# A fused gated-attention and GELU-FFN kernel: two weight pieces fetched ahead of group 1's data, and one addition of the weight conversion done by a transfer

## The chip, the cores and the metric

The kernel runs on one core of one Trainium2 chip. A core has TensorE (PE in the profile; its weight loads are PEld), VectorE (DVE), ScalarE (ACT), GpSimd (POOL) and SyncE (SP), each with an instruction queue of its own that it works off in order, and 16 DMA engines that all queues share. The metric is the device time of one execution in microseconds, lower is better.

## The reference

A gated linear attention with a state of 48 x 48 for each head, over four sequences of 768 steps with eight heads, and behind it a GELU feed-forward layer without bias on the 3072 rows that result. Weights arrive as float64 and are brought to float32 pairs inside the kernel.

```python
for t in range(S):
    state = alpha[:, :, t, :, None] * state + np.einsum('bhd,bhe->bhde', k[:, :, t], v[:, :, t])
    y[:, :, t] = np.einsum('bhd,bhde->bhe', q[:, :, t], state)
...
x = np.ascontiguousarray(attn_out.transpose(0, 2, 1, 3)).reshape(B * S, H * D)
h = x @ w_in
g = 0.5 * h * (1.0 + erf(h * inv_sqrt2))
return (g @ w_out).astype(np.float32)
```

## The kernel before

**Attention.** The 3072 rows are 12 groups of 256 steps, three groups to a sequence. A group has two units of four heads, so there are 24 units; unit n belongs to group n // 2. A unit is loaded by SP in six transfers (decays `ad`, keys `kd`, queries `qd`, two each; with the second unit of a group also the values `vn`). On DVE its *scan part* (L254 to L258) and *back part* (L265, L268) form running products of the decays and scale queries and keys. PE then does *scores* (L284, and L293, which turns the keys), ACT copies the turned keys (`kn`, L300), DVE masks the scores (`ss`, L305), PE does *inside* (L322, L340), DVE sums the state (L357, L359) and carries it on (L364), PE adds the part of the older state, *outer* (L384). ACT casts the result into the feed-forward layer's input x (L426); for the first three groups PE subtracts the cast from the sum (L435) and ACT casts the rest (L441). A few rows of x are moved by six small transfers (L450, *spread*). ACT also checks the range of the decays twice for each unit (L165).

**Feed-forward layer.** The 2048 features are eight blocks. For group g and block f, GEMM1 is 18 matmuls into `hp` (L458), ACT applies GELU twice (L470, L471), the difference of the two is formed (DVE at L476, or PE and ACT at L480 and L484 while g < 3 early on), and GEMM2 is 12 matmuls into `acc` (L497). Evacuations of `acc` into `part` are L511 to L515. A block can be used once its two weight pieces, one of w_in and one of w_out, are converted.

**Weight pieces.** There are 16. Piece n is fetched by SP (L186, into one of three `st` buffers), then: ACT scales the upper half of each float64 (L197, `u`); DVE shifts it (L201), sets the sign (L205, giving `w`), takes the exponents (L215), forms the lower part (L220) and adds it (L230, *add*); ACT casts the sum to the high part (L233, `wih` or `woh`) and DVE subtracts that for the low part (L236, `wil` or `wol`). The lower part was written over the fetched data, which therefore stayed in use until the add.

**What sets the order.** A planner in the kernel (from `plan_unit` and `plan_piece` on) lays all steps out in time from a table of costs, ranks (the string `ORDER`, digits for units, letters for pieces) and dependencies, and the instructions of PE, DVE, ACT and SP are emitted in that order. POOL's follow the order of the program. So a change of ranks, costs or dependencies moves instructions everywhere, and each engine then waits, in its order, for what it needs.

Of the kernel before, what the change touches and what calls it, by code (L numbers as in the profile page):

```python
# [19 lines left out]
SIGN_EXP = -(1 << 23)  # L20
STAGE = 3
WARM = 22
# [8 lines left out]
)  # L31
ORDER = "0 1 2 3 a b c d e f 4 5 g h i j k l m n o p"


@with_exitstack
def gla_then_gelu_ffn(ctx: ExitStack, tc: tile.TileContext, q, k, v, alpha, qg, kg, ag, w_in, w_out, out):
# [154 lines left out]
    def conversion(n):  # L191
        _, hi, lo = pieces[n]
        d = {}

        def scaled():
            d["u"] = stage.tile([P, 2 * DM], F32, tag="u", bufs=1, name=f"u_{n}")
            nc.scalar.activation(d["u"], staged[n].bitcast(F32)[:, 1::2], AF.Copy, scale=2.0**-112)  # L197

        def shifted():
            ui = d["u"].bitcast(I32)  # L200
            nc.vector.tensor_scalar(out=ui, in0=ui, scalar1=3, scalar2=None, op0=ALU.logical_shift_left)  # L201

        def signed():
            d["w"] = stage.tile([P, 2 * DM], F32, tag="w", bufs=2, name=f"w_{n}")
            nc.vector.scalar_tensor_tensor(  # L205
                out=d["w"].bitcast(I32),
                in0=staged[n].bitcast(I32)[:, 1::2],
                scalar=SIGN,
                in1=d["u"].bitcast(I32),
                op0=ALU.bitwise_and,  # L210
                op1=ALU.bitwise_or,
            )

        def exponents():
            nc.vector.tensor_scalar(  # L215
                out=d["u"].bitcast(I32), in0=d["w"].bitcast(I32), scalar1=SIGN_EXP, scalar2=None, op0=ALU.bitwise_and
            )

        def rest():
            nc.vector.scalar_tensor_tensor(  # L220
                out=staged[n].bitcast(F32)[:, 1::2],
                in0=staged[n].bitcast(U16)[:, 1::4],
                scalar=2.0**-36,
                in1=d["u"],
                op0=ALU.mult,
                op1=ALU.mult,
            )

        def whole():
            nc.vector.tensor_tensor(out=d["w"], in0=d["w"], in1=staged[n].bitcast(F32)[:, 1::2], op=ALU.add)  # L230

        def high():
            nc.scalar.copy(flat(hi), d["w"])  # L233

        def low():
            nc.vector.tensor_tensor(out=flat(lo), in0=d["w"], in1=flat(hi).bitcast(F32), op=ALU.subtract)  # L236

        return scaled, shifted, signed, exponents, rest, whole, high, low
# [253 lines left out]
    def gemm2(g, f, ghi, glo, acc, first, last, done, n0=None):  # L492
        for k in range(2):
            for t in range(2):
                for j in range(2):
                    for a, w in (((ghi, wo_hi[f]), (ghi, wo_lo[f])), ((glo, wo_hi[f]),))[k]:
# [5 lines left out]
                            stop=(last and j == 1 and k == 1),  # L502
                        )
        if not last:
            return

        def evacuate():
            o = parts[0 if g == "s" else g % NSB]
            for t in range(2):
                if g in started:  # L510
                    nc.vector.tensor_tensor(out=o[:, t], in0=o[:, t], in1=acc[t], op=ALU.add)  # L511
                elif t == 1 and g == NG - 1:
                    nc.scalar.copy(o[:, t], acc[t])
                else:
                    nc.vector.tensor_copy(o[:, t], acc[t])  # L515
                if g == NG - 1:
                    nc.sync.dma_start(out[g * G + t * C : g * G + (t + 1) * C, :], o[:, t])
            started.add(g)
# [116 lines left out]
    def op(*args, **kw):  # L635
        ops.append(Op(*args, **kw))
        return ops[-1]
# [4 lines left out]
    def plan_unit(n):  # L642
# [10 lines left out]
        old = unit.get(n - NB * NU, {})  # L653
        d["load"] = op("SP", "load", lambda: load_data(g, u), [old.get("outer"), old.get("scores"), old.get("c0"), old.get("c1")] + ([unit[n - NB * NU].get("inside")] if old else []), rank=r - 30, lands=2.8)
        d["scan"] = op("DVE", "scan", start, [d["load"], p.get("q"), p.get("back")], rank=r)
# [11 lines left out]
        d["outer"] = op("PE", "outer", lambda: outside_part(g, u), [d["chain"]], rank=r)  # L667
        if g < NSB:
            for what in ("scores", "inside", "outer"):
                d[what].cost *= SLOW  # L670
# [23 lines left out]
    def plan_piece(n):  # L694
# [3 lines left out]
        r = piece_rank[n]  # L698
        d["get"] = op("SP", "fetch", lambda: fetch(n), [q3.get("c4")], rank=r - 30.5, lands=4.5)
        d["u"] = op("ACT", "u", fns[0], [d["get"], p.get("c3")], rank=-0.5)  # L700
        d["c0"] = op("DVE", "c0", fns[1], [d["u"]], rank=r)
        d["c1"] = op("DVE", "c1", fns[2], [d["c0"], wops.get(n - 2, {}).get("lo")], rank=r)
        d["c2"] = op("DVE", "c2", fns[3], [d["c1"]], rank=r)
        d["c3"] = op("DVE", "c3", fns[4], [d["c2"]], rank=r)
        d["c4"] = op("DVE", "c4", fns[5], [d["c3"]], rank=r)
        d["hi"] = op("ACT", "hi", fns[6], [d["c4"]], rank=-0.4)
# [6 lines left out]

    steps, plan = [], []
    next_f = [0] * NG
# [39 lines left out]
    def gemm1_op(g, t):  # L755
# [4 lines left out]
        if st["first"]:  # L760
            if prev:
                prev["last"] = True
                prev["evac"] = Op("DVE", "part", lambda p=prev: p["out"](), [prev["gemm2"]], rank=-2)
                waiting["DVE"].append(prev["evac"])
            state["run"] += 1
# [163 lines left out]
```

## Time and profile before

| | us |
|---|---|
| median of three runs | 541.49 |
| fastest and slowest of them | 539.23, 543.62 |
| the profiled execution | 538.57 |
| its span, first to last instruction | 537.0 |
| PE busy in the span | 511.0 |
| DVE busy | 302.4 |
| ACT busy | 210.1 |
| POOL busy | 38.6 |

Mean durations of some operations from the profile's groups, in ns:

| operation | ns |
|---|---|
| ACT L470 and L471, GELU | 599 and 595 |
| ACT L197, scaling of a piece | 917 |
| ACT L233, cast of a piece | 837 |
| ACT L300, copy kn | 586 |
| ACT L165, one check, and its read | 722 and 192 |
| ACT L426, cast of x and of z | 482 and 372 |
| DVE L305, mask | 682 |
| DVE L236, low part of a w_out piece | 986 |
| DVE L254 and L265, one scan each of two | 677 and 803 |

Times in the profile count from the span's start. "Busy" leaves the instructions that only issue transfers out. In the timeline a row has its start, its length, the engine, the line of the kernel, what it writes and reads, and in brackets how long its engine was idle before and what ended that. A name like `SPq` is the queue of that engine issuing a transfer. The lines that the argument uses stand in the prediction.

### The profile page before, as it was taken

The page shows a single profiled execution, that of the slowest core. Times are in us where ns is not written, and L with a number is a line of the kernel's source. Part 1 is how long each engine was busy: PE and PEld are TensorE (multiplying, and loading weights), DVE is VectorE, ACT ScalarE, POOL GpSimd, SP SyncE. Part 2 cuts the span into 40 slices and gives each one's busy share as a digit, 9 for nine tenths or more (in the row PEclk, how much of TensorE's full clock was granted, in tenths as well). Part 3 has the DMA queues.
Part 4 walks back from the last instruction along what each step waited for, and adds up shares of the span by engine and source line. Part 5 has one row for each costly group of instructions (what it writes and reads, how often), then busy time and mean ns, then how long its engine had stood idle before and what let it go on. Part 6 is the DMA issues. An engine that isn't in the chain of part 4 may idle for free.

```text
span 537.0 us, 13927 instructions
## 1 busy us (share of the span) xinstructions
PE 511.0 (95%) x5993; PEld 495.7 (92%) x5993; DVE 302.4 (56%) x558; ACT 210.1 (39%) x407; POOL 38.6 (7%) x51
## 2 busy tenths in 40 slices
PE   6667899999999999999999999999999999999995
PEld 6557889999999999999999999999999999999995
DVE  8799999989996976878339145132131121211211
ACT  5347666655435444343243243233232222222221
POOL 5000000000001210111001000000000000000000
PEclk9557999999999999999999999999999999999999
DMA  5838655432004423334022020010010000000001
GB/s 169 287 110 224 180 181 170 129 118 89 1 1 125 151 84 97 99 106 134 0 81 84 2 79 12 1 40 9 1 40 6 0 31 2 30 0 1 31 1 34
DMA packets 20722, 39.49 MB, mean 74 GB/s; under 512 B 4112, under 2 KB 7616, under 8 KB 20656
## 3 DMA queue, kind: packets, MB, share of 16 engines
q1 hardware_dynamic: 19136, 33.93, 21.1%
q0 software_dynamic: 1232, 4.33, 2.4%
q8 instruction: 49, 0.80, 0.7%
q10 hardware_dynamic: 288, 0.30, 0.2%
q14 instruction: 17, 0.14, 0.1%
HBM read 31.46 MB, written 4.72 MB: 67 GB/s over the span
## 4 chain that ended last, share of the span: by engine, by line
PE 86%; DVE 5%; issue 1%; DMA 1%; ACT 1%; SPq 0%
PE hp L458 38%; PE acc L497 37%; PE ybank L384 4%; PE ybank L322 2%; PE s L293 2%; PE s L284 2%; PE ybank L340 2%; DVE state L359 1%; DVE w L205 1%; DVE st L220 1%; DMA qd<-in_qg_dram 1%; DVE rp L265 1%; SPq L153 0%; DVE pp L254 0%; DVE u L215 0%
## 5 line engine op out<-in xcount | busy, mean ns | idle before, releaser
L458 PE MATMUL hp<-x,wih 128*128 128x256 f32 x1152 | 214.1, 285 | 0.0
L458 PEld LDWEIGHTS hp<-x,wih 128*128 128x128 f32 x1152 | 183.5, 192 | 1.1
L458 PE MATMUL hp<-x,wil 128*128 128x256 f32 x576 | 163.3, 284 | 0.0
L476 DVE TENSOR_TENSOR glo<-hp,ghi 128x512 fp32r<-128x512 f32 x87 | 59.9, 688 | 177.5 <-ACT hp L471 177.5
L470 ACT ACTIVATE ghi<-hp 128x512 fp32r<-128x512 f32 x96 | 57.5, 599 | 232.1 <-PE hp L458 231.9
L497 PE MATMUL acc<-woh,ghi 128*128 128x384 f32 x384 | 131.3, 342 | 0.0
L497 PE MATMUL acc<-wol,ghi 128*128 128x384 f32 x384 | 128.6, 335 | 0.0
L458 PEld LDWEIGHTS hp<-x,wil 128*128 128x128 f32 x576 | 110.7, 192 | 0.0
L497 PE MATMUL acc<-woh,glo 128*128 128x384 f32 x384 | 82.1, 334 | 0.0
L497 PEld LDWEIGHTS acc<-woh,ghi 128*128 128x128 f32 x384 | 72.4, 188 | 0.8
L497 PEld LDWEIGHTS acc<-wol,ghi 128*128 128x128 f32 x384 | 72.4, 189 | 0.0
L497 PEld LDWEIGHTS acc<-woh,glo 128*128 128x128 f32 x384 | 67.9, 188 | 0.0
L471 ACT ACTIVATE hp<-hp 128x512 f32<-128x512 f32 x96 | 57.1, 595 | 0.0
L261 POOL TENSOR_TENSOR qd<-qd,pp 128x512 f32<-128x512 f32 x18 | 23.2, 1288 | 224.3 <-DVE pe L255 133.3
L265 DVE TENSOR_TENSOR_SCAN rp<-ad,rp,top 128x255 f32<-128x255 f32 x48 | 36.6, 803 | 0.1
L384 PEld LDWEIGHTS ybank<-qd,state 48*48 48x48 f32 x704 | 23.0, 128 | 12.9 <-DVE state L359 9.5
L384 PE MATMUL ybank<-qd,state 48*48 48x64 f32 x704 | 26.7, 229 | 8.2 <-DVE state L359 8.2
L359 DVE TENSOR_TENSOR state<-ybank,state 128x96 f32<-128x96 f32 x80 | 20.5, 256 | 18.3 <-PE ybank L340 16.1
L254 DVE TENSOR_TENSOR_SCAN pp<-ad,top 128x256 f32<-128x256 f32 x48 | 30.3, 677 | 0.0
L300 ACT COPY kn<-s 128x512 f32<-128x512 f32 x24 | 14.1, 586 | 31.3 <-PE ybank L340 25.5
L521 POOL DMA_DIRECT2D out_dram<-part x11 | 8.3, 752 | 237.4 <-DVE part L515 162.4
L322 PEld LDWEIGHTS ybank<-ss,vn 64*64 64x64 f32 x768 | 14.6, 144 | 11.6 <-DVE ss L305 4.1
(74 smaller groups left out, 428.7 us busy)
## 6 DMA issues: line engine op xcount, KB each, us to landing
st<-in_moe_w_in_dram SPq DMA_DIRECT2D x8, 768.0 KB, 5.2
st<-in_moe_w_out_dram SPq DMA_DIRECT2D x8, 768.0 KB, 4.8
ad<-in_ag_dram SPq DMA_DIRECT2D x48, 96.0 KB, 2.4
kd<-in_kg_dram SPq DMA_DIRECT2D x48, 96.0 KB, 2.3
qd<-in_qg_dram SPq DMA_DIRECT2D x48, 96.0 KB, 3.1
vn<-in_v_dram SPq DMA_DIRECT2D x12, 384.0 KB, 4.3
out_dram<-part POOLq DMA_DIRECT2D x11, 384.0 KB, 3.2
x<-z SPq DMA_DIRECT2D x63, 32.0 KB, 3.0
```

The lines of the kernel that those rows point to most:

```text
L254: nc.vector.tensor_tensor_scan(pp[:, i], at[:, i], top, MID, ALU.mult, ALU.min)
L261: nc.gpsimd.tensor_tensor(out=qt, in0=qt, in1=pp, op=ALU.mult)
L265: nc.vector.tensor_tensor_scan(rp[:, i, G - 2 :: -1], at[:, i, G - 1 : 0 : -1], top[:, 1:], rp[:, i, G - 1 :], ALU.mult, ALU.min)
L300: nc.scalar.copy(d["kn"], d["s"][:, :, 2 * C : 4 * C])
L322: nc.tensor.matmul(ybank[o, b, t : t + CS], lhsT=vn[r, c, e : e + DP], rhs=d["ss"][r, h, 2 * i + c, :], start=(i == 0 and c == 0), stop=(j ...
L359: d["chain"] = nc.vector.tensor_tensor(out=st[j + 1], in0=new, in1=st[j], op=ALU.add)
L384: ins = nc.tensor.matmul(ybank[r, b, t : t + CS], lhsT=states[u][j][r, i], rhs=d["qt"][r, i, j * CS : (j + 1) * CS], start=False, stop=Tru ...
L458: nc.tensor.matmul(hp[:, j, :], lhsT=a[:, j, i * P : (i + 1) * P], rhs=x[:, i, :], start=(j == 0 and i == 0 and n == 0), stop=(i == NK - 1 ...
L470: nc.scalar.activation(ghi, hp, AF.Gelu)
L471: nc.scalar.activation(hp, hp, AF.Gelu)
L476: nc.vector.tensor_tensor(out=glo, in0=hp, in1=ghi.bitcast(F32), op=ALU.subtract)
L497: nc.tensor.matmul(acc[t], lhsT=a[:, j, t * C : (t + 1) * C], rhs=w[:, j, :], start=(first and j == 0 and k == 0 and w is wo_hi[f]), stop= ...
```

## The change

It has five parts.

1. The loads of units 0 and 1 get ranks -40 and -39 and the first two pieces' fetches -33 and -32, so these fetches stand ahead of the loads of units 2 and 3 (group 1). `ORDER` puts pieces a and b ahead of units 2 and 3, c and d ahead of 4 and 5.
2. The add leaves DVE: `w` gets `u` added by a transfer from POOL's queue that accumulates. The lower part is now written into `u`, so the fetched data are free once it is formed, and `u` is in use until the transfer has landed.
3. Buffers: two `st` instead of three, two `u` instead of one, three `w` instead of two. The scaling of piece n now waits for the sum of piece n - 2 instead of the lower part of n - 1.
4. The first evacuation of each of the groups 0 to 2 goes to ACT.
5. The second of the two last stores is issued from ACT's queue. The planner's slow factor for PE holds for the first four units, no longer for six.

```diff
-STAGE = 3
+STAGE = 2
-ORDER = "0 1 2 3 a b c d e f 4 5 g h i j k l m n o p"
+ORDER = "0 1 a b 2 3 c d 4 5 e f g h i j k l m n o p"
...
-            d["u"] = stage.tile([P, 2 * DM], F32, tag="u", bufs=1, name=f"u_{n}")
+            d["u"] = stage.tile([P, 2 * DM], F32, tag="u", bufs=2, name=f"u_{n}")
-            d["w"] = stage.tile([P, 2 * DM], F32, tag="w", bufs=2, name=f"w_{n}")
+            d["w"] = stage.tile([P, 2 * DM], F32, tag="w", bufs=3, name=f"w_{n}")
...
             nc.vector.scalar_tensor_tensor(
-                out=staged[n].bitcast(F32)[:, 1::2],
+                out=d["u"],
                 in0=staged[n].bitcast(U16)[:, 1::4],
...
-            nc.vector.tensor_tensor(out=d["w"], in0=d["w"], in1=staged[n].bitcast(F32)[:, 1::2], op=ALU.add)
+            nc.gpsimd.dma_start(d["w"], d["u"], accum_op=ALU.add)
...
+        EARLY = tuple(range(NSB))
-                elif t == 1 and g == NG - 1:
+                elif g in EARLY or t == 1 and g == NG - 1:
                     nc.scalar.copy(o[:, t], acc[t])
...
-                    nc.sync.dma_start(out[g * G + t * C : g * G + (t + 1) * C, :], o[:, t])
+                    (nc.scalar if t else nc.sync).dma_start(out[g * G + t * C : g * G + (t + 1) * C, :], o[:, t])
...
-        d["load"] = op("SP", "load", lambda: load_data(g, u), [old.get("outer"), old.get("scores"), old.get("c0"), old.get("c1")] + ([unit[n - NB * NU].get("inside")] if old else []), rank=r - 30, lands=2.8)
+        d["load"] = op("SP", "load", lambda: load_data(g, u), [old.get("outer"), old.get("scores"), old.get("c0"), old.get("c1")] + ([unit[n - NB * NU].get("inside")] if old else []), rank=-40.0 + n if n < 2 else r - 30, lands=2.8)
-        if g < NSB:
+        if n < 4:
             for what in ("scores", "inside", "outer"):
                 d[what].cost *= SLOW
...
-        d["get"] = op("SP", "fetch", lambda: fetch(n), [q3.get("c4")], rank=r - 30.5, lands=4.5)
-        d["u"] = op("ACT", "u", fns[0], [d["get"], p.get("c3")], rank=-0.5)
+        d["get"] = op("SP", "fetch", lambda: fetch(n), [q3.get("c3")], rank=-33.0 + n if n < STAGE else r - 30.5, lands=4.5)
+        d["u"] = op("ACT", "u", fns[0], [d["get"], wops.get(n - 2, {}).get("c4")], rank=-0.5)
-        d["c4"] = op("DVE", "c4", fns[5], [d["c3"]], rank=r)
+        d["c4"] = op("POOL", "c4", fns[5], [d["c3"]], rank=r, lands=2.6)
...
-                prev["evac"] = Op("DVE", "part", lambda p=prev: p["out"](), [prev["gemm2"]], rank=-2)
-                waiting["DVE"].append(prev["evac"])
+                again = prev["g"] >= NSB or prev["g"] in evacuated
+                evacuated.add(prev["g"])
+                prev["evac"] = Op("DVE" if again else "ACT", "part", lambda p=prev: p["out"](), [prev["gemm2"]], rank=-2)
+                waiting[prev["evac"].eng].append(prev["evac"])
```

What the planner makes of it shows at three places. The first is ACT's queue from its first work on data (`st` are fetched weights, `s` the scores, `ad` the decays, `x` the layer's input); before:

```order
L300 COPY kn_0_275<-s_0_245 128x512
L165 ACTIVATE junk_319,outside<-ad_118,lo_b 128x512
L197 ACTIVATE u_321<-st_266 128x768
L165 ACTIVATE junk_323,outside<-ad_118,hi_b 128x512
L300 COPY kn_1_353<-s_1_328 128x512
L165 ACTIVATE junk_377,outside<-ad_118,lo_b 128x512
```

And ACT's queue at the same place now:

```order
L197 ACTIVATE u_270<-st_213 128x768
L197 ACTIVATE u_272<-st_223 128x768
L300 COPY kn_0_277<-s_0_249 128x512
L165 ACTIVATE junk_314,outside<-ad_118,lo_b 128x512
L165 ACTIVATE junk_318,outside<-ad_118,hi_b 128x512
L300 COPY kn_1_363<-s_1_322 128x512
```

The scalings of pieces 0 and 1 stand ahead of unit 0's copy; before, the first of them stood between the copies of units 0 and 1. On SP the two fetches stand in the same way right behind the values of group 0.

The second place is DVE's queue behind the mask of unit 0, with the sign step's `w` and the state sums; before:

```order
L305 TENSOR_TENSOR ss_0_277<-s_0_245,mask 128x512
L254 SCALAR_TENSOR_TENSOR pp_0_279<-ad_122,top 128x256 x2
L255 TENSOR_SCALAR pe_0_281<-pp_0_279 128x2
L256 RECIPROCAL rp_0_280<-pe_0_281 128x2
L258 TENSOR_TENSOR qd_124<-qd_124,pp_0_279 128x512
L265 SCALAR_TENSOR_TENSOR rp_0_280<-ad_122,rp_0_280,top 128x255 x2
L268 TENSOR_TENSOR kd_123<-kd_123,rp_0_280 128x512
L357 COPY state_1_146<-ybank 128x96
```

And DVE's queue at the same place now:

```order
L305 TENSOR_TENSOR ss_0_279<-s_0_249,mask 128x512
L201 TENSOR_SCALAR u_270<-u_270 128x768
L205 SCALAR_TENSOR_TENSOR w_316<-st_213,u_270 128x768
L215 TENSOR_SCALAR u_270<-w_316 128x768
L220 SCALAR_TENSOR_TENSOR u_270<-st_213,u_270 128x768
L357 COPY state_1_146<-ybank 128x96
```

Piece 0 takes the place of unit 2's scan and back parts. These now stand behind pieces 0 and 1, and behind them, ahead of unit 2's mask, both low parts.

The third place is PE's queue between the outer parts of units 1 and 2; before:

```order
L284 MATMUL s_1_480<-qd_124,kd_123 64x64 x16
L293 MATMUL s_1_480<-ident,kd_123 128x128 x4
L435 MATMUL ybank<-z_514,minus 128x128 x2
L435 MATMUL ybank<-x_408,minus 128x128 x2
L322 MATMUL ybank<-ss_0_462,vn_121 64x64 x16
L340 MATMUL ybank<-vn_121,kn_0_454 64x48 x16
L384 MATMUL ybank<-qd_124,state_0_145 48x64
```

And PE's queue at the same place now:

```order
L435 MATMUL ybank<-z_499,minus 128x128 x2
L435 MATMUL ybank<-x_378,minus 128x128 x2
L322 MATMUL ybank<-ss_0_478,vn_121 64x64 x16
L340 MATMUL ybank<-vn_121,kn_0_480 64x48 x16
L284 MATMUL s_1_555<-qd_124,kd_123 64x64 x16
L293 MATMUL s_1_555<-ident,kd_123 128x128 x4
L384 MATMUL ybank<-qd_124,state_0_145 48x64
```

The scores of unit 3 have moved from ahead of the subtraction to between the inside part and the outer part of unit 2.

More of the change, by code (lines that the diff above doesn't have):

```diff
@@ L698, in plan_piece @@
         r = piece_rank[n]
-        d["get"] = op("SP", "fetch", lambda: fetch(n), [q3.get("c4")], rank=r - 30.5, lands=4.5)
-        d["u"] = op("ACT", "u", fns[0], [d["get"], p.get("c3")], rank=-0.5)
+        d["get"] = op("SP", "fetch", lambda: fetch(n), [q3.get("c3")], rank=-33.0 + n if n < STAGE else r - 30.5, lands=4.5)
+        d["u"] = op("ACT", "u", fns[0], [d["get"], wops.get(n - 2, {}).get("c4")], rank=-0.5)
         d["c0"] = op("DVE", "c0", fns[1], [d["u"]], rank=r)
-        d["c1"] = op("DVE", "c1", fns[2], [d["c0"], wops.get(n - 2, {}).get("lo")], rank=r)
+        d["c1"] = op("DVE", "c1", fns[2], [d["c0"], wops.get(n - 3, {}).get("lo")], rank=r)
         d["c2"] = op("DVE", "c2", fns[3], [d["c1"]], rank=r)
         d["c3"] = op("DVE", "c3", fns[4], [d["c2"]], rank=r)
-        d["c4"] = op("DVE", "c4", fns[5], [d["c3"]], rank=r)
+        d["c4"] = op("POOL", "c4", fns[5], [d["c3"]], rank=r, lands=2.6)
         d["hi"] = op("ACT", "hi", fns[6], [d["c4"]], rank=-0.4)
@@ L712, in gla_then_gelu_ffn @@
         plan_unit(n)
-    steps, plan = [], []
+    steps, plan, evacuated = [], [], set()
     next_f = [0] * NG
```

## The prediction

> **What bounds the kernel now.** I read the busy times by stretch first, then the chain that ended last, then the timeline of the first 80 us. Columns of the stretches: length, PE, PEld, DVE, ACT and POOL busy, granted TensorE clock, DMA share, GB/s.
>
> ```profile
> 30.00:40.00 10.00, 6.18 (x128) 5.72 (x128) 9.78 (x17) 4.51 (x11) 0.00 (x0) 0.50 0.47 140
> 40.00:50.00 10.00, 6.95 (x65) 6.29 (x69) 8.85 (x18) 7.25 (x13) 0.00 (x0) 0.61 0.76 205
> ...
> 80.00:90.00 10.00, 10.00 (x153) 9.40 (x152) 9.83 (x17) 8.14 (x16) 0.00 (x0) 1.00 0.51 141
> ...
> 400.00:500.00 100.00, 100.00 (x709) 100.00 (x708) 18.87 (x29) 26.18 (x48) 1.45 (x2) 1.00 0.04 12
> ```
>
> From 80 us to the end PE is busy all the time at clock 1.00. Up to 50 us it is busy about two thirds, at half clock, and DVE is nearly full. So the time is a fixed amount of PE work behind a slow start, and the change can only gain or lose in the start, unless it makes PE wait later. The chain (start, length, what):
>
> ```profile
> 42.09 1.95 PE ybank L384 x32
> 44.04 4.07 PE hp L458 x18
> ...
> 77.00 2.15 PE hp L458 x18
> 79.55 2.14 PE acc L497 x12
> ```
>
> The first GEMM1 takes 4.07 us at half clock, a later one 2.15; a GEMM2 takes 2.14. I call the GEMMs by group and feature block, (0,0) the first. I follow the start of the changed kernel with durations from rows (and from the table of means ahead of this part), beside the old one, until both keep PE full. All is against the profiled execution, 538.57 us (span 537.0), 2.9 under the median of the runs, 541.49.
>
> **The change, part by part.** *First pieces ahead.* Two weight loads move on SP from behind the loads of units 2 and 3 (six pair-loads and a value load) to ahead of them, and on ACT both scalings (L197) now stand ahead of the copy kn of unit 0. That copy is waited for by the mask of unit 0 on DVE (both read one PSUM tile), and this by all behind it on DVE and by PE.
>
> ```profile
> 8.00 0.42 SPq L157 DMA_DIRECT2D vn<-in_v_dram  x1
> 13.31 0.69 DVE L268 TENSOR_TENSOR kd<-kd,rp 128x512 f32<-128x512 f32 x1
> 14.59 0.47 SPq L186 DMA_DIRECT2D st<-in_moe_w_in_dram  x1
> 21.24 0.89 ACT L197 ACTIVATE u<-st 128x768 f32<-128x768 f32 x1 [8.52 <-DMA st<-in_moe_w_in_dram]
> 22.74 0.57 ACT L300 COPY kn<-s 128x512 f32<-128x512 f32 x1
> 23.34 0.69 DVE L305 TENSOR_TENSOR ss<-s,mask 128x512 f32<-128x512 f32 x1 [3.48 <-ACT kn L300]
> st<-in_moe_w_in_dram SPq DMA_DIRECT2D x1, 768.0 KB, 6.6
> st<-in_moe_w_out_dram SPq DMA_DIRECT2D x1, 768.0 KB, 8.1
> ...
> st<-in_moe_w_in_dram SPq DMA_DIRECT2D x8, 768.0 KB, 5.2
> out_dram<-part POOLq DMA_DIRECT2D x11, 384.0 KB, 3.2
> ```
>
> In the old kernel ACT waits 8.52 us for the first weight load, and DVE 3.48 behind it. In the new one the second weight load is issued about 9.0 (after the value load at 8.00 and the first weight load). Landing took 8.1 us behind all other loads, 5.2 as the median; I take the middle, 6.65, since half as much is queued ahead: 15.65. Scaling 0.92, copy 0.57: the mask starts at 17.2. DVE is free from 14.0 (13.31 + 0.69), so it waits 3.2 us, at the ends 1.8 and 4.7. The old wait is gone, one of the same size stands earlier.
>
> *DVE up to the first GEMM.* One scan and back part of a unit, from the L254 to the next work, took 4.22; the four operations of a piece 3.05:
>
> ```profile
> 14.52 1.26 DVE L254 TENSOR_TENSOR_SCAN pp<-ad,top 128x256 f32<-128x256 f32 x2
> ...
> 18.74 0.25 DVE L357 COPY state<-ybank 128x96 f32<-128x96 f32 x1
> ...
> 28.33 0.55 DVE L201 TENSOR_SCALAR u<-u 128x768 int32<-128x768 int32 x1
> ...
> 31.38 0.25 DVE L357 COPY state<-ybank 128x96 f32<-128x96 f32 x1
> ...
> L201 DVE TENSOR_SCALAR u<-u 128x768 int32<-128x768 int32 x16 | 9.8, 613 | 0.0
> L215 DVE TENSOR_SCALAR u<-w 128x768 int32<-128x768 int32 x16 | 8.9, 556 | 0.3
> L230 DVE TENSOR_TENSOR w<-w,st 128x768 f32<-128x768 f32 x16 | 15.3, 955 | 0.4
> L515 DVE COPY part<-acc 128x384 f32<-128x384 f32 x23 | 11.7, 550 | 3.3 <-PE acc L497 3.3
> ```
>
> From the mask of unit 0 to that of unit 2 stand now: three masks 2.0, two pieces 6.1, two state sums 2.2 (four operations of about 0.27 each), a carry 0.25, one scan part 4.22, two low parts 1.9: 16.7, so unit 2's mask ends at 33.9. The adds of both pieces (L230, 0.955 each) are gone from this list; they are transfers now. ACT then has copy, check, two casts, check, two rests:
>
> ```profile
> 35.27 0.73 ACT L165 ACTIVATE junk<-ad,hi_b 128x512 bf16<-128x512 f32 x1
> 37.04 0.38 ACT L441 CAST x<-ybank 128x256 fp32r<-128x256 f32 x1
> 14.66 1.14 PE L322 MATMUL ybank<-ss,vn 64*64 64x64 f32 x32 [3.40 <-DMA ad<-in_ag_dram]
> 17.49 1.11 PE L293 MATMUL s<-ident,kd 128*128 128x128 f32 x4
> ```
>
> 0.6 + 0.9 (the check with its read) + 0.75 + 0.9 + 0.75 = 3.9: unit 2's rests end at 37.8 (old: 37.42). PE now runs inside(2) and scores(3) in a row, 3.94 as from 14.66 to 18.60, then outer(2), 1.95: GEMM1 (0,0) starts at 43.7 against 44.04. **-0.3 us.** Unit 3's scan (DVE at 38.4) and state sum (41.1) are in time.
>
> *The clock.* The old PE is idle before 42.09 and then works without a break:
>
> ```profile
> 36.70:42.00 5.30, 2.05 (x65) 1.85 (x64) 5.06 (x12) 1.88 (x4) 0.00 (x0) 0.50 0.92 273
> 42.09:44.00 1.91, 1.91 (x33) 1.76 (x33) 1.11 (x2) 1.88 (x5) 0.00 (x0) 0.50 0.85 202
> ...
> 47.00:47.50 0.50, 0.50 (x4) 0.50 (x4) 0.50 (x1) 0.00 (x0) 0.00 (x0) 0.50 0.72 209
> ...
> 48.00:49.00 1.00, 0.33 (x3) 0.12 (x2) 1.00 (x2) 0.87 (x2) 0.00 (x0) 1.00 0.05 18
> 48.13 0.60 ACT L470 ACTIVATE ghi<-hp 128x512 fp32r<-128x512 f32 x1 [1.94 <-PE hp L458]
> 58.76 0.50 PE L458 MATMUL hp<-x,wih 128*128 128x256 f32 x2
> ```
>
> The clock came up 5.4 to 5.9 us after that start. In the new order PE works without a break from 37.8, so it is up by 43.7 and GEMM1 (0,0) takes 2.15 instead of 4.07. ACT's cast, check and table load (0.6, 0.9, 1.28) behind outer(2) end at 46.5; the first GELU starts there, not at 48.13. **-1.3 us more**; nothing if the break-free run does not come about.
>
> *From there to GEMM1 (0,1).* GELU 1.1, rest 0.5, weight cast 0.85 end at 48.95; DVE, at 48.7, waits 0.25 for that cast, then low part, unit 4's back part (2.05), state sum (1.1): 53.0. Scores, outer, two casts and the subtraction on PE bring GEMM1 (0,1) to 55.85, old 58.76; but inside(4), 1.1, was done before it in the old order and is not in the new, and of the 2.9 - 1.1 = 1.8 the 1.6 above are part. **-0.2.**
>
> *PE filling up.*
>
> ```profile
> 58.76:65.20 6.44, 6.13 (x75) 5.85 (x72) 6.27 (x11) 3.38 (x6) 0.00 (x0) 1.00 0.63 198
> 65.20:72.00 6.80, 6.65 (x109) 5.91 (x111) 6.73 (x11) 3.93 (x8) 0.00 (x0) 1.00 0.46 150
> 72.00:77.00 5.00, 4.29 (x77) 3.91 (x71) 4.83 (x11) 3.91 (x8) 1.27 (x1) 1.00 0.56 174
> ```
>
> The old PE still lost 0.31 + 0.15 + 0.71 = 1.2 us here. In the new one outer(4) waits for its state sum: DVE 53.0 + scan 2.2 + mask 0.6 + carry 0.25 + low part 0.9 + back 2.05 + half a piece 1.5 + sum 0.8 = 61.3; PE is ready at 60.6. It loses 0.7, and behind that DVE is ahead. **-0.5.**
>
> *The sum by a transfer.* No add inside a transfer is in the trace. Nearest below: 384 KB from POOL's queue, 3.2. By bytes read (786,432, the addend and the sum's old value) it is nearest to a weight load, 5.2; the other end is that load's worst, 8.1. I take 5.2. Cover: piece 1's rest ends at 25.75 and its low part's turn on DVE comes at 32.0, so with the cast (0.85) 5.4 us are free; piece 2's, 42.6 to its cast's turn at 48.1, 5.5. POOL has nothing else up to there. At 5.2 it costs **0**; above, each microsecond costs about two. Queued behind such a wait on ACT are casts and GELUs, and PE behind them. The smaller piece buffer (two loads, not three) is covered too: piece 2's load goes out at 20.85, lands by 26.1, and its scaling's turn is then.
>
> The Trainium skill (SBUF — State Buffer, "Summary: rules for kernel authors") speaks against this part: descriptor generation for transfers from GpSimd is starved while DVE is in a 2x or 4x mode, and it advises another queue. Were L201 and L215 such operations and both in the way (0.61 + 0.56), by that rule the transfer would take 6.4, the two places would cost 1.0 and 0.9, and the sum would be -0.6 instead of -2.5. No add beside DVE is in this trace to decide it.
>
> *The rest.* Ten adds after 77 us and the first evacuations (L515, 2 x 0.55 each, now on ACT) leave a DVE that no one waits for once PE is full: 0. The two last stores now issue from two queues:
>
> ```profile
> 531.83 0.84 SPq L517 DMA_DIRECT2D out_dram<-part  x2
> ```
>
> Half of this issue, less ACT's later start: **-0.2.** Together -0.3 - 1.3 - 0.2 - 0.5 - 0.2 = **-2.5**: 536.1 for the profiled execution, 539.0 on the median.
>
> **Rivals.** *All of DVE's relief counts.* The old chain runs over DVE up to 75 us; if the new one does too, six adds (5.7) and one evacuation (1.1) come off it, and the stores' 0.2: -7.0, 534.5. For it: DVE full in the rows above. Against: by the walk ACT and PE end the waits near 37.8, 43.7 and 55.85.
>
> *The transfer is slow.* Place: woh of piece 1 and wih of piece 2 on ACT. At 8.1 us it costs 2.7 + 2.6: +2.8, 544.3. It decides, slower by 1%, from 9.4 us (4.0 + 3.9 - 2.5 = +5.4), 546.9; at 11 us 550. For it: a read, an addition and a write by a path that the trace has not timed, among loads at a DMA share near 0.9. Against: 3.2 for the same bytes stored.
>
> *Nothing moves.* If the clock does not come up early, -1.2: 540.3, the same class.
>
> **How the numbers follow.** A measurement here tells about 1% (5.4 us) from no change. The forecast, a small gain hidden in that, with -0.6 and +2.8 inside: 0.60. DVE's relief in full: 0.23, faster. Slow transfer past 9.4: 0.17, slower. Faster 0.23, same 0.60, slower 0.17. The time is 539.0. The range goes from the fast rival, 534.5, less 2 for the spread of the runs (539.23 to 543.62), to the slow one's threshold, 546.9: 532.5 to 547.0. The likeliest case alone spans -4 (the weight load landing in 5.2) to +2.8: 537.5 to 544.3.
>
> **What would show it.** Right: a DVE wait of about 3 us at the mask of unit 0, released by ACT's kn; the first GEMM1 at 43 to 45 us in about 2.2 us; PE full from about 61; no change after 82. The transfer's time to landing decides cost 0 or not: wrong if ACT's L233 waits for it. Wrong as well if the mask of unit 0 does not wait, or if PE waits for weights after 82 us.

## The result, and the profile after

| | before | after |
|---|---|---|
| median of the runs, us | 540.36 | 557.31 |
| lowest and highest, us | 539.18, 543.62 | 556.63, 558.1 |
| runs | 4 | 4 |
| span of the profiled execution, us | 537.0 | 555.5 |

The ratio is 1.0315, 95% interval 1.028 to 1.0351: 3.2% slower (the kernel before has one run more here than in the table of its times). The forecast was 539.0 us with a range of 532.5 to 547.0, so time and class were both wrong. Medians and ratios, here and below, are of fast runs; one slow run of e10, 988.0 us, is left out.

The stretches of the changed kernel (length, then PE, PEld, DVE, ACT and POOL busy, granted clock, DMA share, GB/s):

```profile
30.00:40.00 10.00, 4.42 (x63) 3.57 (x55) 6.08 (x13) 4.58 (x11) 0.00 (x0) 0.50 0.60 170
40.00:50.00 10.00, 8.11 (x157) 7.07 (x159) 9.67 (x18) 5.82 (x12) 1.44 (x2) 0.78 0.45 111
50.00:60.00 10.00, 6.97 (x112) 5.70 (x112) 6.07 (x14) 2.92 (x4) 0.29 (x1) 0.73 0.96 250
60.00:70.00 10.00, 9.23 (x148) 8.69 (x147) 6.77 (x16) 5.21 (x13) 0.00 (x0) 0.59 0.43 120
...
80.00:90.00 10.00, 10.00 (x172) 9.30 (x167) 6.63 (x13) 7.96 (x16) 1.29 (x1) 1.00 0.70 177
90.00:100.00 10.00, 8.87 (x108) 7.91 (x107) 8.09 (x16) 3.73 (x7) 2.98 (x3) 1.00 0.78 184
100.00:110.00 10.00, 7.83 (x81) 7.02 (x80) 8.34 (x12) 7.90 (x16) 0.86 (x1) 1.00 0.64 188
...
150.00:160.00 10.00, 8.55 (x60) 8.13 (x59) 5.96 (x8) 4.43 (x7) 0.07 (x1) 1.00 0.19 40
160.00:170.00 10.00, 7.37 (x42) 7.20 (x41) 3.78 (x7) 3.39 (x6) 0.78 (x1) 0.86 0.22 41
...
400.00:500.00 100.00, 100.00 (x782) 99.45 (x782) 20.99 (x36) 26.27 (x50) 2.19 (x3) 1.00 0.05 15
```

From 180 us on the two kernels look alike: PE full, clock 1.00. What differs lies ahead of that. The old PE was full from 80 us on. The new one loses 3.3 us between 90 and 110, 0.5 between 130 and 150 and 4.1 between 150 and 170, and the granted clock halves behind the last gap (0.86 in the row of 160 to 170, 0.97 from 170 to 180), which makes about 1.7 us more: 9.6 us after 80. The span grew by 18.5, so the other 8.9 were lost by 80 us. DVE, nearly full before, now has idle time in most stretches.

The waits of ACT up to 180 us (sum, times, longest), and the transfers' time from issue to landing:

```profile
ACT wih L233 <- DMA w<-u: 18.7, 6, 4.2
ACT woh L233 <- DMA w<-u: 14.7, 3, 7.0
ACT u L197 <- DMA w<-u: 12.1, 4, 5.6
```

```profile
st<-in_moe_w_out_dram SPq DMA_DIRECT2D x8, 768.0 KB, 6.9
w<-u POOLq DMA_DIRECT2D x16, 384.0 KB, 7.3
```

ACT stands 45.5 us before sums that have not landed: 33.4 before casts (L233), which need the sum itself, and 12.1 before scalings (L197), which need the buffer `u` that a sum still reads. Half of the sums take over 7.3 us, where the forecast took 5.2. The chain of waits shows how that reaches PE (start, length, what):

```profile
146.81 7.22 DMA w<-u
...
159.94 3.91 DMA w<-u
...
164.61 0.59 ACT ghi L470
...
167.02 3.88 PE acc L497 x12
```

The last piece's sum is issued at 159.94 and lands 3.91 us later. ACT stands 7.0 us before the cast of that piece, the longest of its waits above; the GELU behind the cast comes at 164.61, and the next GEMM2 at 167.02.

### The profile page after: what moved, and what is told of

The parts are those of the page before. It is cut to its first block, busy times and chain, and to the rows that moved or that the text cites. A ratio compares the mean times of both kernels' runs of the same rounds, so it can differ in the third digit from the quotient of the medians.

```text
span 555.5 us, 13974 instructions
## 1 busy us (share of the span) xinstructions
PE 518.4 (93%) x5993; PEld 498.9 (90%) x5993; DVE 282.6 (51%) x534; ACT 210.6 (38%) x413; POOL 53.3 (10%) x67
## 4 chain that ended last, share of the span: by engine, by line
PE 69%; DMA 2%; issue 1%; ACT 1%; DVE 0%; ACTq 0%
PE acc L497 30%; PE hp L458 30%; PE ybank L384 3%; DMA w<-u 2%; PE ybank L322 2%; PE s L293 2%; PE ybank L340 1%; PE s L284 1%; ACT ghi L470 0%; ACT hp L471 0%; DVE glo L476 0%; ACT part L514 0%; DVE part L512 0%; PE tp L869 0%; ACT wih L233 0%
## 5 line engine op out<-in xcount | busy, mean ns | idle before, releaser
L497 PE MATMUL acc<-woh,ghi 128*128 128x384 f32 x384 | 132.7, 346 | 5.0 <-DVE part L512 3.1
L497 PE MATMUL acc<-wol,ghi 128*128 128x384 f32 x384 | 130.2, 339 | 0.0
```

Of the source, the lines that this page charges most:

```text
L497: nc.tensor.matmul(acc[t], lhsT=a[:, j, t * C : (t + 1) * C], rhs=w[:, j, :], start=(first and j == 0 and k == 0 and w is wo_hi[f]), stop= ...
```

## The experiments

Each kernel was timed beside the kernel before on the same chip. The last column is the median less that of the kernel before timed along with it. The intervals leave 1 to 3 us on either side of each difference. Where two of them are set against each other below, it is done before rounding.

| kernel | what it is | median, us | ratio, 95% interval | difference, us |
|---|---|---|---|---|
| after | the change | 557.31 | 1.028 to 1.0351 | +17.0 |
| e1 | sums back on DVE | 544.94 | 1.0052 to 1.0103 | +4.6 |
| e2 | old order, sums by transfer | 559.23 | 1.0292 to 1.0405 | +18.9 |
| e3 | planner reckons 6.5 us | 547.95 | 1.0062 to 1.0177 | +7.7 |
| e4 | copy without addition | 547.23 | one run | +6.9 |
| e5 | new order alone | 541.92 | 1.0004 to 1.0045 | +1.8 |
| e6 | e1 with three buffers | 547.39 | 1.0085 to 1.0146 | +7.3 |
| e7 | evacuations and stores alone | 545.25 | 1.005 to 1.0112 | +5.1 |
| e8 | loads behind the sums | 558.89 | 1.0272 to 1.0362 | +18.8 |
| e9 | sums on DVE, order of after | 549.25 | 1.0154 to 1.0194 | +9.5 |
| e10 | evacuations alone, order of before | 540.04 | 0.9976 to 1.0015 | +0.3 |
| e11 | first six sums by transfer | 548.25 | 1.0131 to 1.0185 | +8.5 |
| e12 | last ten sums by transfer | 554.6 | 1.0235 to 1.0284 | +14.8 |
| e13 | e12, planner reckons 6.5 us | 547.45 | 1.011 to 1.018 | +7.9 |
| e14 | before without the sums | 536.2 | 0.9899 to 0.995 | -3.3 |
| e15 | e11 corrected in three points | 550.69 | 1.0154 to 1.0221 | +11.2 |

Only e4, e9, e10 and e14 keep a written order (e4 and e9 that of the changed kernel, e10 and e14 that of the kernel before). In the others the planner writes it anew, and two of those may differ by some microseconds for that alone, as e7 and e15 show below.

**Is it the transfer, or the rest of the change?** Theory A: the landing time of the transfers, and ACT behind it. Theory B: the early pieces, the buffers or the evacuations.

e1, sums back on DVE:

```diff
-            nc.gpsimd.dma_start(d["w"], d["u"], accum_op=ALU.add)
+            nc.vector.tensor_tensor(out=d["w"], in0=d["w"], in1=d["u"], op=ALU.add)
...
-        d["c4"] = op("POOL", "c4", fns[5], [d["c3"]], rank=r, lands=2.6)
+        d["c4"] = op("DVE", "c4", fns[5], [d["c3"]], rank=r)
```

> The changed kernel with the sum of each piece back on DVE (in place, 0.96 us each) and everything else of the change kept: early pieces, two staging buffers, evacuations on ACT, split last stores. Theory A (the transfer's landing time, 7.3 us median, and ACT's queue standing behind it, make the whole loss): 534 to 541 us, PE without a gap after 82 us, no ACT wait over 3.5 us at a weight cast. Theory B (the early pieces, the third staging buffer taken away or the evacuations on ACT make the loss): at least 550 us. In between, 543 to 549: both have a part.

544.94: 12.4 us of the 17.0 go away, and 4.6 stay. Theory A holds for the larger part. It is not all: it expected 541 at most and no gap of PE, and PE idles 1.9 us between 80 and 90.

e2, the old order with the sums by transfer:

```diff
-ORDER = "0 1 a b 2 3 c d 4 5 e f g h i j k l m n o p"
+ORDER = "0 1 2 3 a b c d e f 4 5 g h i j k l m n o p"
```

The ranks of the first loads are as before, too.

> The changed kernel with the old order of pieces and units and the old ranks of the first loads; sums by transfer, two staging buffers. Theory A: the time stays at 551 to 561 us, with the same ACT waits on the transfers. Theory B with the early pieces as its cause: 545 us or less.

559.23: the early pieces are not the cause of the loss. ACT waits for transfers there as well, 16.0 and 9.2 us at the two kinds of cast.

e9, every engine's order as in the changed kernel, only DVE adds where POOL issued (the planner's line stays):

```diff
-            nc.gpsimd.dma_start(d["w"], d["u"], accum_op=ALU.add)
+            nc.vector.tensor_tensor(out=d["w"], in0=d["w"], in1=d["u"], op=ALU.add)
```

> The changed kernel with every engine's written order kept as it is, the planner still reckoning a transfer, but each sum done by DVE at the place where the transfer was issued. Theory A (the transfer's 7.3 us from issue to landing make the loss): ACT's waits for sums shrink to under 8 us in all and the time falls to 541 to 547 us, as when the planner knows of DVE's sum (544.9). Rival (the order that the planner wrote for a 2.6 us transfer is bad by itself, whoever adds): 552 us or more.

549.25, between the two: 7.5 us less than the change without any new order. ACT waits for no transfer of a sum any more. PE still loses 1.7 us between 80 and 90, and more in two later stretches; in those DVE, which now has the sums and an order written without them, is full:

```profile
90.00:110.00 20.00, 17.98 (x169) 17.33 (x169) 19.59 (x28) 12.15 (x22) 2.59 (x2) 0.91 0.43 137
...
130.00:150.00 20.00, 17.80 (x115) 17.61 (x114) 19.67 (x28) 7.40 (x12) 0.90 (x1) 0.91 0.20 68
```

So the transfer costs 7.5 us in this order, and 12.4 with an order made for the one or the other.

**Which of the sixteen sums?** e11 sends the first six by transfer, e12 the last ten (there with `n >= 6`):

```diff
-            nc.gpsimd.dma_start(d["w"], d["u"], accum_op=ALU.add)
+            if n < 6:
+                nc.gpsimd.dma_start(d["w"], d["u"], accum_op=ALU.add)
+            else:
+                nc.vector.tensor_tensor(out=d["w"], in0=d["w"], in1=d["u"], op=ALU.add)
...
-        d["c4"] = op("POOL", "c4", fns[5], [d["c3"]], rank=r, lands=2.6)
+        d["c4"] = op("POOL" if n < 6 else "DVE", "c4", fns[5], [d["c3"]], rank=r, lands=2.6 if n < 6 else 0.0)
```

> The changed kernel with only the first six pieces summed by transfer, the last ten on DVE. With all sixteen PE was 8.9 us behind the kernel before at 80 us and lost 9.6 more after; with none it is 544.9. If both halves cost by themselves: 549 to 553 us. If lateness of the first six runs on into everything behind: 555 us or more. If only the last ten cost: 547 us or less.

> The changed kernel with only the last ten pieces summed by transfer, the first six on DVE. The forecast took nothing for these ten, since PE is full there. If that held: 547 us or less, as with none. If the last ten make PE run out of weights between 90 and 170 us by themselves: 550 us or more, with PE idle 4 us or more in that stretch.

Over e1, the first six cost 3.8 us and the last ten 10.2, together 14.0, where all sixteen cost 12.4. The larger part lies where the forecast took nothing; the 3.8 are not more than an order written anew can make (548.25 lies between what e11's theories expected). In e12 (columns as above; an inserted line moves L233 to L236):

```profile
110.00:130.00 20.00, 18.32 (x156) 17.52 (x154) 16.70 (x26) 10.69 (x20) 2.98 (x3) 1.00 0.59 151
130.00:150.00 20.00, 15.69 (x95) 15.51 (x96) 14.29 (x22) 9.19 (x16) 3.84 (x4) 0.89 0.59 147
```

```profile
ACT wih L236 <- DMA w<-u: 16.3, 5, 4.2
```

PE idles 1.7 and 4.3 us in stretches that were full before.

**ACT's order, or late pieces?** e3 has only the planner's number for the transfer changed, e13 the same for the last ten:

```diff
-        d["c4"] = op("POOL", "c4", fns[5], [d["c3"]], rank=r, lands=2.6)
+        d["c4"] = op("POOL", "c4", fns[5], [d["c3"]], rank=r, lands=6.5)
```

> The changed kernel with a planner that reckons 6.5 us from issue to landing of a sum, not 2.6: the order written for ACT then sets casts later and other work ahead of them. If the loss is ACT standing in order before a cast whose sum has not landed (45 us of such waits up to 180 us), those waits fall below 15 us and the time to 545 us or less. If the pieces themselves come too slowly, whatever stands ahead of them, the waits fall but PE still runs out of weights after 90 us: 549 to 557 us.

> The changed kernel with the last ten pieces summed by transfer and the planner reckoning 6.5 us for each, not 2.6. With 2.6 it took 554.6 us, 9.7 more than with none by transfer. If the 9.7 us are ACT standing in order before casts whose sums have not landed, 547 us or less. If the pieces come too late whatever the order: 551 us or more.

e3 takes 547.95: 9.3 us less than the change, by a number in the planner, with the sums landing in 6.6 us as a median. ACT stands before no cast any more, only before scalings that need a sum's buffer:

```profile
ACT u L197 <- DMA w<-u: 12.7, 4, 4.5
```

e13 takes 547.45, 6.9 less than e12. Most of the cost is thus ACT standing in order before casts that were written too early. e3's time lies between what its two theories expected, and e13's just above the bound of the first. What is left over e1 is 3.0 us for e3 and 3.3 for e13; that can be lateness of the pieces themselves or the order written anew, and no run tells these apart.

**Why does a sum take 7 us?** e4 copies and does not add:

```diff
-            nc.gpsimd.dma_start(d["w"], d["u"], accum_op=ALU.add)
+            nc.gpsimd.dma_start(d["w"], d["u"])
```

> The changed kernel with a plain copy in place of the adding transfer, same size, queue, place and waits; the addition is left out. If the addition inside the transfer makes it slow, the copy lands in a median of 3.2 to 4.5 us (the stores of 384 KB from the same queue take 3.2) and the time is 545 us or less. If the packets stand behind the weight load that is released by the same DVE operation, it lands in 6 to 7 us and the time is 552 us or more.

It landed in a median of 6.1 us, as the theory of the queue has it, but took 547.23 us, a time that this theory did not expect. Both have a share in the 7.3 us. The time fell much more than the landing, 10.1 us in the same written order (one run): ACT's waits before these transfers come to 29.8 us instead of 45.5, PE idles 3.9 us behind 80 us instead of 7.9, and the granted clock, once up, does not fall again while PE is full. It is 1.00 between 60 and 80 us, where the change has 0.79:

```profile
60.00:80.00 20.00, 18.59 (x329) 17.23 (x330) 18.18 (x35) 15.24 (x32) 2.36 (x3) 1.00 0.70 211
```

How the 10.1 us divide among these, no run shows. The queue's rows, of the change and of the copy (packets, MB, share of the 16 engines over the span):

```profile
q0 software_dynamic: 3536, 10.62, 8.1%
```

```profile
q0 software_dynamic: 2512, 10.62, 5.5%
...
w<-u POOLq DMA_DIRECT2D x16, 384.0 KB, 6.1
```

The stores alone are 2.4% of 537.0 us in the profile of the kernel before. Less those, a sum keeps all 16 engines busy for 2.0 us and a copy for 1.1; the fastest sum landed after 3.9 us, the fastest copy after 2.6. The rest is waiting. Packets around a sum issued at 106.71, half a microsecond behind a weight load released by the same DVE operation (L220): first from 107.25 to 109.50, then from 109.50 to 112.50; and a sum with nothing beside it, from 160.94 to 163.85:

```profile
q1 hardware_dynamic: 190, 0.58, 88.5%
```

```profile
q0 software_dynamic: 143, 0.39, 68.4%
q1 hardware_dynamic: 82, 0.20, 22.4%
```

```profile
q0 software_dynamic: 144, 0.39, 74.4%
```

While 190 packets of the loads' queue (q1) go, the sum (q0) gets none. The first packet of the lone one started 1.4 us after its issue, and it landed after 3.9. The other's first packet started 2.9 us after its issue, so it was held back for 1.5 us more; it then shared the engines with the rest of the load, and landed after 6.3:

```profile
st<-in_moe_w_in_dram SPq DMA_DIRECT2D x1, 768.0 KB, 4.9
w<-u POOLq DMA_DIRECT2D x1, 384.0 KB, 6.3
```

```profile
w<-u POOLq DMA_DIRECT2D x1, 384.0 KB, 3.9
```

The Trainium skill (DMA: Bandwidth & Descriptors, "Queues, rings and completion order") says that a DMA engine goes in turn between the queues it has work for, and drains a whole packet of one, typically 9 to 17 descriptors, before it switches. The 190 packets of the profile are 12 for each engine: if they are descriptors of the page, this is a single turn and the trace agrees; if they are its packets, it does not. No run here tells which.

e8 issues the loads from POOL too, each behind the sum:

```diff
-        nc.sync.dma_start(staged[n].rearrange("p (two e) -> p two e", two=2), pieces[n][0])
+        (nc.sync if n < STAGE else nc.gpsimd).dma_start(staged[n].rearrange("p (two e) -> p two e", two=2), pieces[n][0])
...
-        d["get"] = op("SP", "fetch", lambda: fetch(n), [q3.get("c3")], rank=-33.0 + n if n < STAGE else r - 30.5, lands=4.5)
+        d["get"] = op("SP" if n < STAGE else "POOL", "fetch", lambda: fetch(n), [q3.get("c3")], rank=-33.0 + n if n < STAGE else r + 0.1, lands=4.5)
```

> The changed kernel with the weight loads from the third on issued from POOL's queue, each behind the adding transfer that the same DVE operation releases. If the transfer lands late because the load's packets go ahead of it (packets of the add at 107 us began only when most of the load's were through), it lands in a median of 5 us or less, and the time falls to 553 us or less though the loads come later. If it is slow by itself or by the other loads, the median stays at 6.5 us or more and the time at 555 us or more.

```profile
w<-u POOLq DMA_DIRECT2D x16, 384.0 KB, 4.9
st<-in_moe_w_in_dram POOLq DMA_DIRECT2D x7, 768.0 KB, 8.3
st<-in_moe_w_out_dram POOLq DMA_DIRECT2D x7, 768.0 KB, 8.4
```

The sums land in 4.9 us, so the load ahead is most of what kept them. The time does not fall: the loads now take 8.4, and ACT's waits for loads are 29 us instead of 11.7. One of the two is late whichever goes first.

**The 4.6 us that are not the transfer.** e5 is the kernel before with the new order, with the new ranks of the first loads and the planner's slow factor for four units:

```diff
-ORDER = "0 1 2 3 a b c d e f 4 5 g h i j k l m n o p"
+ORDER = "0 1 a b 2 3 c d 4 5 e f g h i j k l m n o p"
```

> The kernel before with the new order alone: the first two pieces ahead of group 1's loads, their two loads issued behind unit 1's, three staging buffers, the sum on DVE, evacuations on DVE. With the sum on DVE the whole rest of the change lost 4.6 us, 0.77%. If the early pieces make that loss (the mask of unit 2 and GEMM1 (0,0) come later), 543 to 547 us. If the forecast's terms for this part hold (-0.3, -1.3, -0.2, -0.5), 536 to 540 us, and the loss lies with the buffers or the evacuations.

e6 is e1 with the old buffers, and with the dependencies on them:

```diff
-STAGE = 2
+STAGE = 3
...
-            d["u"] = stage.tile([P, 2 * DM], F32, tag="u", bufs=2, name=f"u_{n}")
+            d["u"] = stage.tile([P, 2 * DM], F32, tag="u", bufs=1, name=f"u_{n}")
...
-            d["w"] = stage.tile([P, 2 * DM], F32, tag="w", bufs=3, name=f"w_{n}")
+            d["w"] = stage.tile([P, 2 * DM], F32, tag="w", bufs=2, name=f"w_{n}")
```

> The changed kernel with the sum on DVE and the old buffers: three staging buffers, one u, two w. If the loss of 4.6 us comes from the third staging buffer taken away (ACT waits 17 us for weight loads in the first 180 us with two), 541 us or less and these waits below 10 us. If it comes from the order or the evacuations, 543 to 547 us.

e7 is the kernel before with the change's lines for the evacuations and the last stores, planned anew:

```diff
-                elif t == 1 and g == NG - 1:
+                elif g in EARLY or t == 1 and g == NG - 1:
...
-                    nc.sync.dma_start(out[g * G + t * C : g * G + (t + 1) * C, :], o[:, t])
+                    (nc.scalar if t else nc.sync).dma_start(out[g * G + t * C : g * G + (t + 1) * C, :], o[:, t])
...
-                prev["evac"] = Op("DVE", "part", lambda p=prev: p["out"](), [prev["gemm2"]], rank=-2)
+                prev["evac"] = Op("DVE" if again else "ACT", "part", lambda p=prev: p["out"](), [prev["gemm2"]], rank=-2)
```

> The kernel before with two parts of the change alone: each group's first evacuation on ACT (four of them), the last two stores from two queues. The forecast took 0 and -0.2: 539 to 541 us. If ACT, which holds the GELUs, is late by two evacuations of 0.86 us in a row there, 542 us or more.

The order costs 1.8 (between what e5's theories expected), the evacuations with the split stores 5.1, and the old buffers do not help (e6 is 2.6 slower than e1, in an order of its own). 1.8 and 5.1 are more than the 4.6 to be explained, so the parts do not add up. e10 then swaps the engine of the first evacuations and leaves every order as it was:

```diff
-                elif t == 1 and g == NG - 1:
+                elif g in range(NSB) or t == 1 and g == NG - 1:
```

> The kernel before with the first evacuations (three pairs of copies before all weights are there) on ACT at the same place of the written order; nothing replanned, last stores untouched. If ACT's time is what the evacuations cost (545.25 us when replanned): 543 us or more. If that loss came from the other order that the planner wrote, the time stays at 539 to 541.5 us.

540.04, no change. So ACT has the time for the evacuations; e7's loss most likely comes with the order that the planner wrote when one operation moved (the split stores, which e10 lacks, lie at the end of the span and were not tried alone). Where the 4.6 us lie stays open.

**What could be gained at all?** e14 leaves the sums out of the kernel before, in its written order:

```diff
-            nc.vector.tensor_tensor(out=d["w"], in0=d["w"], in1=staged[n].bitcast(F32)[:, 1::2], op=ALU.add)
+            pass
```

> The kernel before, same written order, with the sixteen sums on DVE left out (the lower part of each weight piece is not added). This is the most that taking the sum off DVE can bring in that order: sixteen times 0.955 us less on DVE, and a transfer of no time at all. If DVE's relief counts in full as the fast rival had it, 534 us or less. If PE is the bound from 80 us on and only the start can gain: 536 to 539.5 us.

536.2 us, 3.3 less; PE is full from 80 us on as before, and the gain lies ahead of that (between 40 and 60 us the granted clock averages 0.87, before 0.80):

```profile
40.00:60.00 20.00, 15.89 (x296) 14.46 (x295) 18.26 (x37) 14.22 (x27) 0.00 (x0) 0.87 0.77 211
80.00:90.00 10.00, 10.00 (x174) 9.28 (x172) 8.81 (x17) 7.25 (x14) 0.00 (x0) 1.00 0.47 158
```

e15 puts together what the runs spoke for: e11 with 6.5 us reckoned, evacuations (the diff of e7 undone) and last stores as before:

```diff
-        d["c4"] = op("POOL" if n < 6 else "DVE", "c4", fns[5], [d["c3"]], rank=r, lands=2.6 if n < 6 else 0.0)
+        d["c4"] = op("POOL" if n < 6 else "DVE", "c4", fns[5], [d["c3"]], rank=r, lands=6.5 if n < 6 else 0.0)
```

> The changed kernel with what the runs so far speak for: only the first six sums by transfer, the planner reckoning 6.5 us for them, evacuations on DVE and last stores as before. If the three corrections add up (3.3 us for the six, 2.8 and more for the evacuations as replanned, from 548.25): 540 to 543 us, level with the kernel before. If an order written anew costs its own few microseconds whatever is in it: 544 us or more.

550.69, and slower than e11. The corrections do not add up, and no version here that does all of the sums beats the kernel before.

## Why the prediction was wrong, point by point

**First pieces ahead, -0.3: the place was right, the sum was not.** The wait that the forecast set at the mask of unit 0 (3.2, ends 1.8 to 4.7) is there with 2.68, and the second load was in by 15.25, forecast 15.65. The start of the changed kernel:

```profile
16.72 0.69 DVE L305 TENSOR_TENSOR ss<-s,mask 128x512 f32<-128x512 f32 x1 [2.68 <-ACT kn L300]
...
20.78 1.28 POOL L230 DMA_DIRECT2D w<-u  x1 [12.31 <-DVE state L357]
...
25.27 1.11 SPq L186 DMA_DIRECT2D st<-in_moe_w_out_dram  x1
25.56 0.85 POOL L230 DMA_DIRECT2D w<-u  x1 [3.51 <-DVE u L220]
...
34.32 0.83 ACT L233 CAST woh<-w 128x768 fp32r<-128x768 f32 x1 [4.11 <-DMA w<-u]
...
36.05 0.68 DVE L305 TENSOR_TENSOR ss<-s,mask 128x512 f32<-128x512 f32 x1
...
40.51 1.13 PE L322 MATMUL ybank<-ss,vn 64*64 64x64 f32 x32 [0.74 <-ACT x L441]
...
45.40 0.50 PE L458 MATMUL hp<-x,wih 128*128 128x256 f32 x2
...
48.28 0.60 ACT L470 ACTIVATE ghi<-hp 128x512 fp32r<-128x512 f32 x1
...
53.98 0.83 ACT L233 CAST wih<-w 128x768 fp32r<-128x768 f32 x1 [4.10 <-DMA w<-u]
...
63.66 0.73 PE L458 MATMUL hp<-x,wih 128*128 128x256 f32 x2
```

Unit 2's mask ends at 36.73, not 33.9, because DVE stood behind the cast of piece 1, and that behind its sum. GEMM1 (0,0) starts at 45.40, forecast 43.7. With the sums on DVE its first matmul starts at 44.26 in e5, 0.3 us later than the old one at 43.97, not 0.3 earlier.

**The clock, -1.3: it was up in time, in part by luck, and the gain went elsewhere.** GEMM1 (0,0) ran at full clock and took 2.4 us by its matmuls' first start and last end, 4.13 before. But the run without a break that the forecast asked for did not come about: PE idled 0.74 us up to 40.51, and the granted clock was 0.50 until 44.3 us and full from there, 3.8 us behind that gap and not 5.4 to 5.9. And ACT, behind a copy, two checks, a cast and the table load, reached the first GELU at 48.28, not 46.5; before it was 48.13.

**The sum by a transfer, cost 0: this is the step that failed, first in its size.** The forecast took 5.2 us to landing, between 3.2 and 8.1, against a cover of 5.4 for piece 1 and 5.5 for piece 2. Piece 1's rest ended at 25.24 and its cast ran at 34.32: 9.1 us. Piece 2's ended at 45.23, the cast ran at 53.98: 8.8 us. Both overran the cover, by 3.7 and 3.3 us, and ACT stood 4.1 us each time. GEMM1 (0,1), forecast for 55.85, came at 63.66. The nearest rows were taken for size in bytes; that the same DVE operation releases a 768 KB load, which goes ahead, stood in the order and was not drawn on (the rows at 25.27 and 25.56).

As far as e1, in an order of its own, can show, what such an overrun costs was priced about right. By the forecast's own rule these two are 7.0 us. The change stands 8.9 us behind the kernel before at 80 us, and e1, with the sums on DVE, about 2.7 (its span is 6.3 us longer, and some 3.6 of that come behind 80), so the transfers made about 6.2 there. And 541.49 - 2.5 + 7.0 = 546.0 is still inside the range: the time left it by the next term.

**The rest, ten more adds at 0: the same step failed a second time, and for more.** The words "a DVE that no one waits for once PE is full" looked at the engine that was relieved. The engine that was burdened is ACT: its queue holds each cast ahead of GELUs, so a sum that lands later than the planner thought can delay PE. The change itself said `lands=2.6` for its planner; the forecast took 5.2 and did not ask what an order written for 2.6 does at the other places. The last ten cost 10.2 us (e12 over e1), of which 6.9 went when the planner reckoned with the landing (e13). In the change 9.6 us were lost behind 80 us. The evacuations' 0 was right for the instructions (e10) and not for the kernel (e7): the forecast did not price that the whole order is written anew.

**The rule that was weighed.** By the Trainium skill (SBUF — State Buffer, "Summary: rules for kernel authors") descriptors for POOL's transfers are starved beside some DVE operations, which would have made 6.4 us. The first sum was issued at 20.78, the row above, with an operation on DVE inside that time that may be of that kind (0.55 us, where L220 takes 0.96 for as many elements). So was the third, at 45.53. Behind these rows stand the issue times of all sixteen (ns, least, median and most):

```profile
21.41 0.55 DVE L201 TENSOR_SCALAR u<-u 128x768 int32<-128x768 int32 x1
...
45.53 0.90 POOL L230 DMA_DIRECT2D w<-u  x1 [19.11 <-DVE u L220]
45.75 0.55 DVE L201 TENSOR_SCALAR u<-u 128x768 int32<-128x768 int32 x1
```

```profile
L230 POOL DMA_DIRECT2D w<-u x16: 828/850/1276, 20.8 to 159.9; - x16
```

The trace bears the rule out at most once: the first issue took 1.28 us where the median is 0.85, the third 0.90 with the same operation wholly inside it. That is 0.4 us, in one of sixteen. The 7.3 us are near the 6.4 for another reason, the load ahead: without that the sums land in 4.9 (e8).

**The rivals.** "The transfer is slow" named the place (ACT's L233) and the sign. Its price was wrong: +2.8 at 8.1 us and 550 only at 11, since it counted two of sixteen places; at a median of 7.3 the change was at 557.31. "Nothing moves" set its 540.3 on a clock that stays down; it came up. "All of DVE's relief counts", -7.0, was out of reach: e14 has the full relief and no transfer, in the old order, and gains 3.3. The forecast's own -2.5 for the start is of that size, but e5 gains nothing from the new order. There DVE still has the sums; no run has the new order with DVE relieved and no transfer. What the profile was to show as wrong, ACT's L233 waiting for the transfer and PE waiting for weights after 82 us, both came.

## What to carry to other kernels

An operation that is moved from an engine to a transfer is paid at its consumer: set its landing, behind every load that the same event releases, against what the consumer's in-order queue has to do meanwhile, and do that for all its places, not for the first two. A planner needs that landing time too: 6.5 in place of 2.6 us in one line was worth 9.3 us here. And where a planner writes the order, judge an edit once with the old order kept (e9, e10): otherwise its own effect and that of the new order, 2 to 5 us here, can't be told apart.

## What the hardware showed that was not expected

A burst of one queue's load held back another queue's issued transfer for 1.5 us (190 packets to none, above). And a short idle time of PE cost more than itself. In the changed kernel, with PE busy in the second column and the granted clock third from the end:

```profile
54.00:56.00 2.00, 0.65 (x4) 0.64 (x4) 1.16 (x2) 2.00 (x3) 0.00 (x0) 0.86 1.05 279
56.00:58.00 2.00, 0.39 (x6) 0.11 (x7) 1.96 (x4) 0.10 (x1) 0.00 (x0) 0.99 1.03 354
58.00:60.00 2.00, 2.00 (x36) 1.58 (x36) 1.91 (x5) 0.81 (x1) 0.00 (x0) 0.50 0.57 135
...
68.00:70.00 2.00, 2.00 (x93) 1.93 (x89) 0.73 (x4) 0.94 (x2) 0.00 (x0) 0.95 0.51 144
```

PE was busy for 1.0 of 4 us, and then had half clock for 10 us, in which it was busy for 9.2: by this about 4.6 us of work that came late (an estimate, half of 9.2), more than the 3.0 us that PE was idle. The Trainium skill (TensorE: Matmul & The Clock Gate, "What's actually happening") says that the clock halves after an idle window of about 3.4 us, and comes back after as long a busy one. The trace agrees with the first roughly, since PE was not wholly idle in those 4 us. The way back took longer here: PE was busy from 57.9 to 62.0 and still at half clock, idle for 0.8 us, and busy again from 62.75; the clock came back at about 68.2.
